# Three of sixteen activation sums of a block: from VectorE subtractions to in-place adding DMAs

## The chip, the cores and the metric

The kernel runs on one core of a Trainium2 chip. The metric is device time in microseconds (us) of one launch. Before the change three runs gave 2333.43, 2333.84 and 2334.41 us, median 2333.84.

## What is computed

A lightweight convolution (each of 8 heads has 7 softmax-normalised taps, causal in the sequence) runs over 8 x 4096 tokens of 192 channels, and its result goes through a two-layer block with a SiLU between, all in float32:

```python
w = np.exp(weight - weight.max(-1, keepdims=True)); w = w / (w.sum(-1, keepdims=True) + 1e-09)
x = einsum('hk,bskhg->bshg', w, windows_of_7(x_padded)).reshape(32768, 192)
h = x @ w_in            # 192 -> 2048
g = h * (1 / (1 + np.exp(-h)))
out = g @ w_out         # 2048 -> 192
```

## The kernel before

**Blocks.** The 32768 tokens are 32 blocks of 1024, each two token halves `n` of 512. The 2048 inner channels are four groups `j` of 512, and a group is two halves `a` of two chunks `e` of 128. Block 0 is multiplied plainly (`up_plain`, `down_plain`); blocks 1 to 31 use schemes with fewer multiplications.

**Up.** Per block and group, 20 products (`P0` to `P19`, `product`, L656) of 64 rows each go into PSUM banks named b0 to b6. Between them stand copies and additions in `micro`: copies `k`, `u`, `h` on ScalarE (L687, L689), or on VectorE (L678, L681) if their name is in `ON_DVE`; additions `i`, `j` on VectorE (L694); and the SiLU `S13` to `S20` on ScalarE (L691), which writes g. g lies in SBUF as eight tiles `gs[b, j, a]` of 128 partitions x (n, e, 512); a tile is written anew in each block. `of(a, n)` is one half of such a tile, 128 x 1024. `S14` and `S16` write `of(0, 1)`; `S18` and `S20` write `of(1, 1)`.

**Sums.** A 2x2 scheme for the second multiplication needs four sums of g per group, `t.j0` to `t.j3` (`sum_g`, L711), so 16 a block, each one VectorE subtraction of 128 x 1024. They go into two rotating tiles, `t0` (sums 0 and 1) and `t1` (sums 2 and 3). Sum 0 reads `of(0, 1)` and `of(0, 0)`; sum 1 reads `of(1, 1)` and sum 0; sum 2 reads `of(1, 1)` and `of(0, 1)`; sum 3 reads `of(1, 0)` and sum 1.

**Down.** `out_slot` (L746) issues slots `Di.je` (i from 0 to 5, group j, chunk e), each of four products side by side on 32 columns of the array. They accumulate in banks acc0 to acc5. Slot 3 alone reads sum 2 (beside sum 3). Slot 5 moves a quarter of the columns. A float32 matmul is two instructions in the profile, so a `P` is 2 of them and a `D` is 8.

**Merge and store.** `merge` (`M1` to `M7`, L823, VectorE) adds the accumulators, with ScalarE copies `x`, `y`, `z` (L803 to L811) beside it; `o` (`turn_out`, L835) transposes; `st` stores through SP's queue.

**The next block's input** is made meanwhile: `ld` loads through SP's queue, `i` transposes (L548, VectorE), `ha` takes over the last columns of the block before (a small copy on Pool, L569, and a DMA on SP's queue), `v` convolves (18 instructions on VectorE, L582; three on ScalarE, L579), `sp` spreads the result by DMAs (L599) and `w` adds windows (L607), which the products read.

**Order.** The order is written out by hand: `START` for the first blocks and `PLAN` for each later one are lists of tokens, and every engine executes its own in list order. `+` names the next block's token, `-` and `=` in START those of one and two blocks earlier. The lists fix the order within an engine only; between engines it is semaphores. `dp` are pieces of block 0's `down_plain` (L765), `cp` copies of its result, `go` half passes of `combine` (weight sums on VectorE), `co` calls of `combine_out` (sums of w_out). `D3` slots of the last block wait until the token `CLOSING` is done, and `finish` closes the last block. `TOUCHES` counts the uses after which a tile is free again.

Pool has little to do after the weights are made: the small `ha` copy once a block. DMAs issued by Pool exist only at the start (`w_other<-w_own`, L456).

Of the kernel before, what the change touches and what calls it, by code (L numbers as in the profile page):

```python
# [12 lines left out]
ALU = mybir.AluOpType  # L13
# [4 lines left out]
def kernel(  # L18
# [12 lines left out]
    nc = tc.nc  # L31
# [16 lines left out]
    NJ = NM // 2  # L48
# [41 lines left out]
    )  # L90
    START = (
# [1031 lines left out]
```

## Time and profile before

| what | us |
|---|---|
| profiled execution, whole | 2334.11 |
| its span, first to last instruction | 2332.4 |
| matmuls (PE) busy | 2324.2 (100%) |
| VectorE (DVE) busy | 2178.5 (93%) |
| ScalarE (ACT) busy | 1330.8 (57%) |
| Pool busy | 53.7 (2%) |
| the sums, VectorE L711, 496 instructions | 302.5 + 300.6 |
| granted TensorE clock | 0.999 |

A share near 100% for PE says that some matmul is nearly always in flight; it does not say that the matmuls follow each other as closely as they can, because the end of each is modelled and covers the start of the next. So time is read from the distances between starts. In groups of instructions, a row reads: line, engine, operation, output tile <- inputs, shape, count, then total busy time and mean ns of one, then the engine's idle time before these and what ended it. PEld is the weight load of a matmul, which runs ahead of it. POOLq and SPq are the issuing of DMAs.

### The profile page before, as it was taken

The page shows a single profiled execution, that of the slowest core. Times are in us where ns is not written, and L with a number is a line of the kernel's source. Part 1 is how long each engine was busy: PE and PEld are TensorE (multiplying, and loading weights), DVE is VectorE, ACT ScalarE, POOL GpSimd, SP SyncE. Part 2 cuts the span into 40 slices and gives each one's busy share as a digit, 9 for nine tenths or more (in the row PEclk, how much of TensorE's full clock was granted, in tenths as well). Part 3 has the DMA queues.
Part 4 walks back from the last instruction along what each step waited for, and adds up shares of the span by engine and source line. Part 5 has one row for each costly group of instructions (what it writes and reads, how often), then busy time and mean ns, then how long its engine had stood idle before and what let it go on. Part 6 is the DMA issues. An engine that isn't in the chain of part 4 may idle for free.

```text
span 2332.4 us, 43764 instructions
## 1 busy us (share of the span) xinstructions
PE 2324.2 (100%) x17382; PEld 921.5 (40%) x17382; DVE 2178.5 (93%) x3045; ACT 1330.8 (57%) x2523; POOL 53.7 (2%) x84
## 2 busy tenths in 40 slices
PE   9999999999999999999999999999999999999998
PEld 5344343334333344333344333443334433334433
DVE  8999999999999999999999999999999999999996
ACT  5356655566654576545666555665457654566654
POOL 4200000000000000000000000000000000000000
PEclk9999999999999999999999999999999999999999
DMA  7211221212212222212122122221221221212211
GB/s 159 57 37 26 53 53 30 50 32 49 53 37 43 44 37 53 45 37 50 28 53 53 30 49 35 46 53 39 40 51 30 53 49 34 50 28 53 53 33 22
DMA packets 451246, 106.55 MB, mean 46 GB/s; under 512 B 423585, under 2 KB 428705, under 8 KB 451041
## 3 DMA queue, kind: packets, MB, share of 16 engines
q1 hardware_dynamic: 447392, 101.78, 23.3%
q8 instruction: 136, 2.23, 0.4%
q0 software_dynamic: 448, 1.58, 0.3%
q10 hardware_dynamic: 3200, 0.39, 0.1%
q14 instruction: 70, 0.57, 0.1%
HBM read 31.46 MB, written 25.17 MB: 24 GB/s over the span
## 4 chain that ended last, share of the span: by engine, by line
PE 95%; DVE 1%; SPq 0%; DMA 0%; issue 0%; ACT 0%; ACTq 0%
PE ps L746 48%; PE ps L656 47%; SPq L599 0%; DVE t L711 0%; DMA nat<-in_x_dram 0%; DVE win L607 0%; DVE u L678 0%; DVE w_other L257 0%; SPq L289 0%; DVE w_own L257 0%; DVE cmb L257 0%; DVE ps L694 0%; ACT u L257 0%; DVE g L694 0%; DVE wx L257 0%
## 5 line engine op out<-in xcount | busy, mean ns | idle before, releaser
L656 PE MATMUL ps<-win,w_own 64*128 64x512 f32 x1488 | 661.4, 598 | 0.8 <-DVE win L607 0.5
L746 PE MATMUL ps<-g,wo 128*32 128x512 f32 x2976 | 661.5, 592 | 0.0
L746 PE MATMUL ps<-t,wo 128*32 128x512 f32 (+1 forms) x4528 | 511.3, 447 | 0.0
L656 PE MATMUL ps<-dup,w_own 64*128 64x512 f32 x1240 | 492.5, 594 | 0.2 <-ACT ps L689 0.2
L746 PE MATMUL ps<-t,wx 128*32 128x512 f32 x2976 | 484.7, 592 | 0.0
L691 ACT ACTIVATE g<-ps 128x512 f32<-128x512 f32 x620 | 367.1, 599 | 186.6 <-DVE g L694 113.9
L656 PE MATMUL ps<-dup,w_other 64*128 64x512 f32 x1240 | 460.0, 595 | 0.0
L656 PE MATMUL ps<-win,w_other 64*128 64x512 f32 x992 | 444.6, 595 | 0.0
L694 DVE TENSOR_TENSOR g<-g,ps 128x512 f32<-128x512 f32 x496 | 331.3, 683 | 54.4 <-PE ps L656 35.4
L582 DVE SCALAR_TENSOR_TENSOR nat<-xt,turned,nat 128x512 f32<-128x512 f32 x558 | 378.2, 746 | 3.9 <-ACT nat L579 1.6
L808 ACT COPY yx<-ps 32x512 f32<-32x512 f32 x150 | 84.3, 579 | 516.7 <-PE ps L746 514.9
L656 PEld LDWEIGHTS ps<-win,w_own 64*128 64x128 f32 x1488 | 246.6, 186 | 211.4 <-issue 120.3
L711 DVE TENSOR_TENSOR t<-g,t 128x1024 f32<-128x1024 f32 x248 | 302.5, 1220 | 16.9 <-PE ps L746 9.6
L711 DVE TENSOR_TENSOR t<-g 128x1024 f32<-128x1024 f32 x248 | 300.6, 1212 | 13.3 <-PE ps L746 13.1
L746 PEld LDWEIGHTS ps<-t,wo 128*32 128x32 f32 x4528 | 175.1, 110 | 248.4 <-issue 189.9
L694 DVE TENSOR_TENSOR ps<-u,ps 128x512 f32<-128x512 f32 x372 | 255.3, 687 | 11.8 <-ACT u L687 5.2
L656 PEld LDWEIGHTS ps<-dup,w_own 64*128 64x128 f32 x1240 | 195.5, 186 | 142.7 <-issue 77.2
L746 PE MATMUL ps<-g,wx 128*32 128x512 f32 x1488 | 245.7, 592 | 0.0
L691 ACT ACTIVATE g<-g 128x512 f32<-128x512 f32 x372 | 220.8, 625 | 27.1 <-DVE g L694 23.6
L689 ACT ACTIVATE ps<-ps 128x512 f32<-128x512 f32 x372 | 214.5, 584 | 36.0 <-DVE ps L694 19.0
L746 PEld LDWEIGHTS ps<-g,wo 128*32 128x32 f32 x2976 | 173.1, 110 | 148.0 <-issue 147.2
L656 PEld LDWEIGHTS ps<-dup,w_other 64*128 64x128 f32 x1240 | 167.8, 186 | 131.3 <-ACT ps L689 50.3
(102 smaller groups left out, 1826.3 us busy)
## 6 DMA issues: line engine op xcount, KB each, us to landing
dup<-nat SPq DMA_DIRECT2D x221, 128.0 KB, 2.3
nat<-in_x_dram SPq DMA_DIRECT2D x382, 64.0 KB, 2.4
out_dram<-t SPq DMA_DIRECT2D x372, 64.0 KB, 2.0
win<-nat SPq DMA_DIRECT2D x124, 128.0 KB, 2.4
raw<-in_moe_w_out_dram SPq DMA_DIRECT2D x8, 384.0 KB, 3.9
raw<-in_moe_w_in_dram SPq DMA_DIRECT2D x12, 192.0 KB, 5.0
w_other<-w_own POOLq DMA_DIRECT2D x8, 192.0 KB, 5.6
raw<-in_moe_w_in_dram SPq DMA_DIRECT2D x6, 128.0 KB, 3.4
```

What stands on the lines that cost most here:

```text
L582: nc.vector.scalar_tensor_tensor(out=dst, in0=src, scalar=tap, in1=dst, op0=ALU.mult, op1=ALU.add)
L656: nc.tensor.matmul(at(b, "bank", to, g), raw(g, w, e), rows(slot_of(b, x_), e), start=first, stop=True, skip_group_check=True,)
L689: pin(nc.scalar.activation(seen[to], seen[u], AF.Copy, scale=-1.0))
L691: pin(nc.scalar.activation(seen[to], seen[u], AF.Silu, scale=float(sign)))
L694: pin(nc.vector.tensor_tensor(seen[to], seen[u], seen[v], op=op))
L711: pin(nc.vector.tensor_tensor(t[i // 2][:, i % 2, :], u, v, op=ALU.subtract))
L746: nc.tensor.matmul(acc[SQ * q : SQ * q + SQ, to], lhs[:, e, SQ * k : SQ * k + SQ], rhs[:, e, ts(q, TB // 4) if i == 5 else to], start=firs ...
L808: pin(nc.scalar.copy(to, acc(3 * (name[0] == "x") + k)[n:P, :]))
```

## The change

Sum 2 of groups 0, 1 and 2 is no longer a VectorE instruction: Pool's queue issues a DMA that reads `of(1, 1)`, 128 x 1024 float32 (512 KB), and adds it into `of(0, 1)` where that lies. Group 3, and groups 2 and 3 of the last block, do the same addition on VectorE in place. `t1` thus holds sum 3 only, and slot 3 reads `of(0, 1)` of the g tile instead.

Such a DMA can add but not subtract, so signs move: all sums are now additions, `combine_out` swaps an addition and a subtraction in the weights, and `M2`, `M5` and three additions of `finish` become subtractions, with the same operands.

`PLAN` and `START` are replaced by other orders of (but for the five tokens that change the side of a block's border) the same tokens, `ON_DVE` grows from ten names to twelve, `TOUCHES` of `t1` goes from 8 to 7, and `CLOSING` becomes `S16.3`.

```diff
-    ON_DVE = ('h15.3', 'h18.0', 'k12.0', 'k12.1', 'k12.3', 'k8.0', 'u10.1', 'u10.2', 'u10.3', 'u6.2')
-    CLOSING = "S14.3"
+    ON_DVE = ('h15.3', 'h18.2', 'k12.0', 'k12.1', 'k5.3', 'k8.0', 'k8.1', 'k9.0', 'k9.3', 'u4.2', 'u4.3',
+              'u6.2')
+    BY_DMA = (0, 1, 2)
+    CLOSING = "S16.3"
...
-        t = {k: sums_of(b, j, k) for k in ((0,), (0,), (1,), (0, 1))[i]}
+        t = {k: sums_of(b, j, k) for k in ((0,), (0,), (), (0, 1))[i]}
+        if i == 2:
+            to, u = of(0, 1), of(1, 1)
+            if j in BY_DMA and not (b == NB - 1 and j >= NJ // 2):
+                pin(nc.gpsimd.dma_start(out=to, in_=u, accum_op=ALU.add))
+            else:
+                pin(nc.vector.tensor_tensor(to, u, to, op=ALU.add))
+            return
         u, v = (
             (lambda: (of(0, 1), of(0, 0))),
             (lambda: (of(1, 1), t[0][:, 0, :])),
-            (lambda: (of(1, 1), of(0, 1))),
+            None,
             (lambda: (of(1, 0), t[0][:, 1, :])),
         )[i]()
-        pin(nc.vector.tensor_tensor(t[i // 2][:, i % 2, :], u, v, op=ALU.subtract))
+        pin(nc.vector.tensor_tensor(t[i // 2][:, i % 2, :], u, v, op=ALU.add))
...
-            7: lambda: (a_[1][0], t(2)),
+            7: lambda: (a_[1][0], gs[b, j, 0][:, 1]),
...
-            "M2": lambda: (c[3], c[1], acc(1)[0:n, :]),
+            "M2": lambda: (c[3], acc(1)[0:n, :], c[1]),
...
-            "M5": lambda: (c[3], c[2], acc(4)[0:n, :]),
+            "M5": lambda: (c[3], acc(4)[0:n, :], c[2]),
...
-        pin(nc.vector.tensor_tensor(out_, u, v, op=ALU.add))
+        op = ALU.subtract if name in ("M2", "M5") else ALU.add
+        pin(nc.vector.tensor_tensor(out_, u, v, op=op))
```

The part of PLAN that the sums stand in, before and after (VectorE's and Pool's tokens of it alone; those in brackets are now Pool's):

```
before  +i15_11.1 +u10.2 +t.00 +u6.2 +j6.2 +i15_f.2 +t.02 +u10.3 +j6.3 +t.01 +t.03 +i15_f.3 +j10.2 +i18_10.2
        +j10.3 +i18_10.3 +ze.0 +t.10 +i15_11.2 +i17_f.2 +i17_f.3 +t.11 +t.13 +t.20 +t.21 +i15_11.3
        (next list) i.1 i.0 i.2 t.12 t.23 t.22 v.01 v.21 ...
after   +i15_11.1 +k5.3 +u6.2 +h18.2 +j6.2 +i15_f.2 +t.00 +j6.3 +k9.3 +t.01 +i15_f.3 +t.03 +j10.2 +i18_10.2
        [+t.02] +ze.0 +j10.3 +i18_10.3 +i17_f.2 +t.10 +i17_f.3 +i15_11.2 [+t.12] +t.11 +t.13 +i15_11.3
        +t.20 +t.21 [+t.22] (next list) i.1 i.0 i.2 t.23 v.21 v.22 ...
```

And TensorE's tokens of the same part:

```
before  ... +P13.3 +P10.3 +P4.3 +P15.2 +P9.3 +P15.3 +D3.01 +D2.01 +P12.2 +P14.2 +P12.3 +P14.3 +D3.00 +D4.00
        +D5.01 +D4.01 +D5.00 +D2.00 +D2.11 +D2.10 +D4.10 ... (next list) D3.11 D5.10 D3.10 D5.20 ... D3.20 D3.21
after   ... +P13.3 +P10.3 +P12.2 +P15.2 +P4.2 +P15.3 +D2.01 +D4.01 +D2.00 +P12.3 +P14.2 +P4.3 +P14.3 +D4.00
        +D5.01 +D3.00 +D5.00 +D0.30 +D3.01 +D4.10 +D1.31 +D4.11 +D2.11 +D2.10 +D0.00 +D0.21 +D3.10 ...
        (next list) D5.20 D4.21 D4.20 D3.21 ... D3.20
```

In START, the three tokens `go.0`, `go.2`, `go.1` stand on VectorE before the window `w.5` of block 1 and `go.3` some instructions behind it; before the change it was `go.2`, `go.3`, `co.0` before and `go.0` behind, `go.1` further on.

More of the change, by code (lines that the diff above doesn't have):

```diff
@@ L232 @@
                't0': 7,
-               't1': 8,
+               't1': 7,
                'acc0': 10,
@@ L494, in combine_out @@
         x_ = [wx[j][:, i, :, :] for i in range(3)]
-        vec.tensor_tensor(x_[0], a_(1, 0), a_(1, 1), op=ALU.add)
+        vec.tensor_tensor(x_[0], a_(1, 0), a_(1, 1), op=ALU.subtract)
         vec.tensor_tensor(x_[1], x_[0], a_(0, 0), op=ALU.subtract)
-        vec.tensor_tensor(x_[2], a_(0, 1), x_[1], op=ALU.subtract)
+        vec.tensor_tensor(x_[2], a_(0, 1), x_[1], op=ALU.add)
         vec.tensor_tensor(a_(1, 0), a_(0, 0), a_(1, 0), op=ALU.subtract)
@@ L934, in part, with add @@
             return t[SQ * k : SQ * k + SQ, :]
-        def add(out_, u, v):
-            vec.tensor_tensor(out_, u, v, op=ALU.add)
+        def add(out_, u, v, op=ALU.add):
+            vec.tensor_tensor(out_, u, v, op=op)
         def store(i, cols):
@@ L976, in finish @@
         act.copy(part(y, 2), acc(2)[n:P, :])
-        add(c[1], c[2], acc(1)[0:n, :])
+        add(c[1], acc(1)[0:n, :], c[2], ALU.subtract)
         add(c[0], c[0], y[0:n, :])
@@ L981, in finish @@
         add(c[1], c[1], acc(4)[0:n, :])
-        add(c[3], c[2], acc(4)[0:n, :])
+        add(c[3], acc(4)[0:n, :], c[2], ALU.subtract)
         act.copy(part(x_, 1), acc(4)[n:P, :])
@@ L994, in finish @@
                     )
-            add(c[3][:, cols], c[3][:, cols], p7[0:n, cols])
+            add(c[3][:, cols], c[3][:, cols], p7[0:n, cols], ALU.subtract)
             add(c[2][:, cols], c[2][:, cols], p7[0:n, cols])
```

190 rows, old and new, of tables (PLAN, START) are left out of this document.

## The prediction

> **What bounds the kernel now.** I read the page's first part, then the chain that ended last in order of time, to see at what pace the blocks follow each other; then the timeline of TensorE, VectorE and ScalarE over one block, to see where that pace is not the matmuls' own. The page, and four pieces of the chain:
>
> ```profile
> PE 2324.2 (100%) x17382; PEld 921.5 (40%) x17382; DVE 2178.5 (93%) x3045; ACT 1330.8 (57%) x2523; POOL 53.7 (2%) x84
> PE 95%; DVE 1%; SPq 0%; DMA 0%; issue 0%; ACT 0%; ACTq 0%
> ...
> 858.21 34.50 PE ps L746 x368
> 892.72 33.29 PE ps L656 x151
> 926.00 1.85 PE ps L746 x16
> 927.86 1.92 PE ps L656 x8
> 929.77 34.50 PE ps L746 x368
> ```
>
> Columns of the pieces: start, length, what. Block follows block at 71.56 us (929.77 - 858.21), all of it TensorE. In the timeline a product starts 0.429 us after the one before and a full slot takes twice that, 0.858. A block has 80 products (34.3 us), 40 full slots (34.3) and 8 quarter slots (1.7): 70.4 us. What is left, 1.17 us a block, is all that any edit off TensorE can win there: 36 us in 31 blocks, 1.5%. Most of it is the four changes a block between products and slots; the new list has four as well (its products stand in two runs of 76 and 4). What remains is waits. One is seen in TensorE's rows, its weight loads and the two engines behind it (products `P13.3`, `P10.3`, and the end of the first run at `P15.3`):
>
> ```profile
> 1565.29 1.22 DVE L711 TENSOR_TENSOR t<-g 128x1024 f32<-128x1024 f32 x1
> 1566.42 0.68 DVE L678 COPY u<-ps 128x512 f32<-128x512 f32 x1
> 1567.07 0.70 DVE L694 TENSOR_TENSOR ps<-u,ps 128x512 f32<-128x512 f32 x1
> 1567.86 1.07 ACT L689 ACTIVATE ps<-ps 128x512 f32<-128x512 f32 x2 [0.22 <-DVE ps L694]
> 1568.49 0.18 PEld L656 LDWEIGHTS ps<-dup,w_own 64*128 64x128 f32 x1 [0.64 <-ACT ps L689]
> 1568.51 0.68 PE L656 MATMUL ps<-win,w_own 64*128 64x512 f32 x1
> 1569.03 0.59 PE L656 MATMUL ps<-win,w_own 64*128 64x512 f32 x1
> 1570.74 0.59 PE L656 MATMUL ps<-dup,w_other 64*128 64x512 f32 x1
> 1570.88 0.59 PE L656 MATMUL ps<-dup,w_own 64*128 64x512 f32 x1
> 1571.40 1.07 PE L746 MATMUL ps<-t,wo 128*32 128x512 f32 x8
> 1574.64 0.59 PE L656 MATMUL ps<-win,w_own 64*128 64x512 f32 x1
> 1575.17 1.07 PE L746 MATMUL ps<-t,wo 128*32 128x512 f32 x8
> ```
>
> The first three rows are `t.02`, `u10.3` and `j6.3` without a gap; ScalarE's `k9.3` waits for `j6.3`, `P13.3`'s weights wait for `k9.3`, and 1568.51 to 1569.03 is 0.52 instead of 0.43. So a sum that this change takes off VectorE stands in a chain that holds TensorE, for 0.09 us. At the end of the first run the second half of `P15.3` starts 0.14 late, and the way to the slots is 0.66 (1570.74 to 1571.40), against 0.53 at the end of the second (1574.64 to 1575.17): 0.13 more. VectorE's own share over a whole block, 1503.68 to 1575.24, is 67.41 us of 71.56 in the stretches view: 4.1 us free.
>
> For the adding DMA the nearest rows are Pool's eight early transfers, and plain ones of SP:
>
> ```profile
> w_other<-w_own POOLq DMA_DIRECT2D x8, 192.0 KB, 5.6
> raw<-in_moe_w_out_dram SPq DMA_DIRECT2D x8, 384.0 KB, 3.9
> nat<-in_x_dram SPq DMA_DIRECT2D x382, 64.0 KB, 2.4
> ...
> L456 POOL DMA_DIRECT2D w_other<-w_own x8: 518/639/876, 22.6 to 42.3; - x8
> DMA to landing us min/median/max: 3.2/5.6/6.7
> ```
>
> **The change part by part.**
>
> *VectorE loses 92 sums* (31 blocks x 3, less one), of 1.22 us by the row of L711: 112 us. `ON_DVE` gives it two copies more a block, 62 x 0.68 = 42 us, and takes 62 x 0.59 = 37 us from ScalarE. VectorE ends 70 us lighter, some 90% busy. None of that is on TensorE's path by itself; it counts only where a wait on VectorE holds a matmul.
>
> *The wait at P13.3.* In the new order `t.02` and `u10.3` are gone ahead of `j6.3`, `k9.3` follows it on VectorE, and `P13.3` stands eight products behind `P6.3`, whose result `j6.3` adds, instead of six. From `i15_11.1` to `j6.3` VectorE has six instructions instead of seven, with one sum of 1.2 us less. I take the wait as gone: 30 x 0.09 = -2.7 us (bounds 0 and -2.7).
>
> *The late second half of P15.3.* It shows 0.13 x 30 = 3.9 us. ScalarE's `k17.3` is next to it, in a queue that loses two copies a block; what holds it I can't tell for sure. Bounds 0 and -3.9, I take half: -2.0.
>
> *Late blocks.* In the chain the distance from one L746 x368 piece to the next is 71.56 in most blocks and more in a few (1073.67 - 1001.34 = 72.33; 1503.68 - 1431.75 = 71.93); the excess over 71.56 adds up to 2.0 us. The one at 1489 to 1497 runs through VectorE, with both `t.00` and `t.02` in it. Bounds 0 and -2.0, I take -1.5.
>
> *The DMAs: 92 issues on Pool's queue.* Nothing is queued behind them there but `ha`'s small copy, 0.51 us, which has to be done when `i.2` and its DMA are; `t.22` is issued when `t.20` is done, at about 1580.9, and `ha` is needed after 1583.5, so it passes. The issuing itself takes Pool 0.65 us and nobody waits for Pool. Landing: from 192 KB at 5.6; from 64 to 384 KB SP's rows grow by 1.5 us, 4.7 ns a KB, so 512 KB adds 320 x 4.7 = 1.5, and reading the destination too adds 512 x 4.7 = 2.4: 9.5 us. Bounds: 5.6 (if the bytes cost nothing), and 5.6 x 512/192 = 14.9 (if all of it goes by bytes); I take 9.5, since the rows of SP say that most of a transfer is fixed. When is it needed? `t.10` ended at 1574.78; the new order puts `i17_f.2` ahead of it, so 1575.3. The second run of products ends where it did plus one slot (three slots stand in the gap instead of two), less the waits: `D4.00` at 1576.0. Before `D3.10` come eleven full slots and two quarters, 9.9 us: 1585.9. That leaves 10.6 us, so 9.5 is hidden, with 1.1 to spare. For `t.02` it is about the same: `t.00`, which ended at 1563.45, has four more instructions of 0.65 ahead of it and ends near 1566.1, `D3.00` starts at 1577.1, 11.0. For `t.22` it is some 19 (`D3.21` stands 17 full slots behind `D3.10`). The DMA engines are 23% busy; loads, spreads and stores each wait in SP's queue for their own inputs long before they are needed, except the spreads just ahead of the windows, and those run 10 us after `t.22` has landed. Price: 0, by this cover.
>
> That this cover is thin, one sentence of the Trainium skill says too: "SBUF — State Buffer", "Summary: rules for kernel authors", holds that making the descriptors of a Pool-issued DMA is starved while VectorE runs in its faster two-port modes. The rows show eight issues of 518 to 876 ns beside a VectorE that was 53.31 of the first 60 us busy, so such a delay is at most 0.36 us each here, and by the rule the landing would be 9.9, still inside 10.6.
>
> *A tile that is free later.* `of(0, 1)` is now read by `D3` until TensorE is through; the next block's `S14`, `S16` write it more than 30 us on. Price 0.
>
> *Signs.* An addition for a subtraction is the same VectorE instruction with the same operands: 0.
>
> *START.* `w.5`, which `P1.0` needs, now stands behind 21 half-pass instructions of the weight sums instead of 15 and `co.0` (four of 0.35): 21 x 0.44 - (15 x 0.44 + 1.4) = +1.2 us; against that 7 of them (3 us) leave the place between `w.5` and the first copies, and two transposes (1.4) come in. `go.3` (3 us) comes behind `j4.0`, earlier than `go.1` did. Bounds -1.5 and +3.2; VectorE is 39.42 of 40 us busy from 60 to 100, so this shows. I take +1.0.
>
> *Sum.* The profiled execution took 2334.11 us, 0.27 over the median: 2334.11 - 2.7 - 2.0 - 1.5 + 1.0 = 2328.9, and against the median 2328.6.
>
> **The rivals.**
>
> *No change that counts* (within 0.2%, 4.7 us, about what a measurement of this kernel can tell from none). VectorE was not the bound, 4.1 us a block were free, and its relief becomes idle time: P13.3 is held by the next thing (`k9.3` itself), the half of P15.3 stays, and START costs 1 to 3 us. For it: only 0.22 us a block is named above. Then 2334 - 2.7 + 2 = 2333.
>
> *The adding DMA lands after TensorE asks for it* (slower). Place: `D3.10`, and `D3.00` with it. It decides at 10.6 us from the end of `t.10` to the landing: each us beyond costs 31 us in all, since TensorE has nothing else in its order. For it: an addition in flight is in no row of this trace, and the bound of 14.9 lies beyond. Against it: the median of 5.6 and the 6.7 at most, in a stage where the DMA engines were 72% busy. At 12 us: +1.4 x 31 - 5 = +38, 2372.
>
> *The new order makes a wait of its own* (slower). `t.13` ends at 1575.3 + 1.3 + 2.4 = 1579.0 and `D4.10` starts at 1579.9, which leaves 0.9 (1579.7 and 1580.8 before, 1.1); and `D0.30`, at 1578.1, waits for `S17.3`, whose input now comes behind `t.10` on VectorE. If either slips past that by 0.4 us in each block: 31 x 0.4 = +12, less 5: 2341.
>
> *More than named.* All waits but the four changes go, 0.5 us a block: 2334 - 15 - 2 = 2317.
>
> **How the numbers follow.** Forecast, with the last rival at its far end: 0.42, own range 2321 to 2329. No change: 0.25, 2329 to 2338. Late DMA: 0.20. A wait of the new order: 0.13, 2339 to 2350. The range 2321 to 2350 holds all but the far end of the first (0.03) and the late DMA beyond 11.3 us (0.15). Faster 0.42, same 0.25, slower 0.33.
>
> **What would show it.** Right: pieces of the chain at 71.3 to 71.5 us a block; the L711 row of `t<-g` down by 92; no wait of PEld or PE by a DMA at L746; 1568.51 to 1569.03 again 0.43. Wrong: idle time of PEld at L746 ended by a DMA whose issue is at the new Pool line, with landings over 10.6 us; or the block's pace unchanged and VectorE's idle time 2 us larger; or, for START, less matmul work started between 100 and 110 us than the 7.1 us of now (by the slots above).

## The result and the profile after

The changed kernel takes 2339.69 us (median of 10 runs, 2338.83 to 2340.97); the kernel before, run beside it, 2334.14 us (2333.13 to 2335.45). The ratio is 1.0024, with a 95% interval of 1.0014 to 1.0034: slower by 5.5 us, where 2328.6 was forecast. The profiled execution took 2339.14 us, its span 2337.4 us, against 2332.4 us before. Lines of the page after, parts 1, 4 and 5:

```profile
PE 2328.0 (100%) x17382; PEld 954.1 (41%) x17382; DVE 2122.7 (91%) x3015; ACT 1292.0 (55%) x2461; POOL 136.1 (6%) x176
PE 95%; DVE 4%; issue 0%; DMA 0%; SPq 0%; ACT 0%; DVEq 0%; ACTq 0%
L584 DVE SCALAR_TENSOR_TENSOR nat<-xt,turned,nat 128x512 f32<-128x512 f32 x558 | 391.2, 747 | 68.0 <-ACT nat L581 62.5
```

VectorE is lighter, as meant, and yet its share of the chain that ended last rose from 1% to 4%. The row to see first is L584, the convolution `v`: VectorE now idles 68.0 us in front of it. (What this idle time is worth, the experiments have to say.) The adding DMAs themselves land in 4.6 us (median); the new DMA line, by its own view:

```profile
L710 POOL DMA_DIRECT2D g<-g x92: 853/862/972, 134.4 to 2295.8; - x92
DMA to landing us min/median/max: 4.5/4.6/6.3
```

**Where the 5.0 us of the span went.** I took the start of `P7.0` in each block as its border. From the span's start to the block that begins at 320 us the changed kernel is 0.4 us quicker; the 27 blocks after that take 1937.8 us against 1934.2 (+3.6); from the last block's `P7.0` to the end it is 80.0 against 78.2 (+1.8).

In the middle two things oppose each other. The shortest block, which is also the commonest, fell from 71.56 to 71.49 us, since the forecast wait at `P13.3` is gone: 27 x 0.07 = -2.0. But the excess of the longer blocks over that rose from 2.1 to 7.6 us in all, +5.5. Before, 4 of the 27 are over 0.2 us longer than the shortest; after, 13 are. The stretches view of one undisturbed block of after (columns: length, then busy time and instructions of PE, PEld, DVE, ACT and POOL, clock, DMA share, GB/s):

```profile
1514.26:1585.75 71.49, 71.49 (x547) 28.94 (x543) 65.23 (x92) 40.53 (x77) 3.21 (x4) 1.00 0.35 64
```

VectorE is busy for 65.23 us of a block (67.41 before), the DMA engines for 35% of it.

**The late blocks, read in the trace.** The next block's input ends with the transpose `i.2`; then `ha.0`'s DMA on SP's queue brings 4.5 KB (the halo), and only then can ScalarE start the first convolutions `v.20`, `v.00`, whose results VectorE's `v.21` and `v.01` add to. The timeline of before, at a typical block whose `i.2` ended at 939.09:

```profile
939.01 1.18 DVE L711 TENSOR_TENSOR t<-g 128x1024 f32<-128x1024 f32 x1
940.12 1.21 DVE L711 TENSOR_TENSOR t<-g,t 128x1024 f32<-128x1024 f32 x1
941.25 1.22 DVE L711 TENSOR_TENSOR t<-g 128x1024 f32<-128x1024 f32 x1
942.38 2.19 DVE L582 SCALAR_TENSOR_TENSOR nat<-xt,turned,nat 128x512 f32<-128x512 f32 x3
...
941.20 1.95 ACT L579 ACTIVATE nat<-xt,turned 128x512 f32<-128x512 f32 x3 [2.28 <-DVE t L711]
```

VectorE fills the time of the halo's flight with `t.12`, `t.23` and `t.22`, and goes on at 942.38 without a gap. After, `t.12` and `t.22` are DMAs, and `t.23` stands there alone. A late block and the one behind it (their `i.2` ended at 867.61 and 940.33):

```profile
867.54 1.22 DVE L720 TENSOR_TENSOR t<-g,t 128x1024 f32<-128x1024 f32 x1
872.61 1.54 DVE L584 SCALAR_TENSOR_TENSOR nat<-xt,turned,nat 128x512 f32<-128x512 f32 x2 [3.85 <-ACT nat L581]
871.86 1.95 ACT L581 ACTIVATE nat<-xt,turned 128x512 f32<-128x512 f32 x3 [7.40 <-DMA xt<-xt]
...
940.25 1.23 DVE L720 TENSOR_TENSOR t<-g,t 128x1024 f32<-128x1024 f32 x1
943.48 2.87 DVE L584 SCALAR_TENSOR_TENSOR nat<-xt,turned,nat 128x512 f32<-128x512 f32 x4 [2.00 <-ACT nat L581]
942.72 1.95 ACT L581 ACTIVATE nat<-xt,turned 128x512 f32<-128x512 f32 x3 [5.55 <-DMA xt<-xt]
```

In the second VectorE idles 2.0 us; in the first the halo is late, ScalarE starts 4.25 us after `i.2` instead of 2.4, and VectorE idles 3.85. I call a halo late when ScalarE's first `v` starts over 2.9 us after the end of `i.2`: 2 of 27 blocks before, 5 of 28 after. The waits view gives the sums over the run, first of before, then of after (us in total, times, longest):

```profile
ACT nat L579 <- DMA xt<-xt: 30.8, 11, 7.1
DVE nat L582 <- ACT nat L579: 2.5, 3, 0.9
```

```profile
ACT nat L581 <- DMA xt<-xt: 124.2, 22, 7.5
DVE nat L584 <- ACT nat L581: 63.3, 30, 4.0
```

What follows behind the convolution has little room. In the new order `t.30` and `t.31` stand among the `v`, so `v.16` ends 17.9 us after `i.2` (15.6 before); its spread `sp.4` lands at 20.1, just when the window sum `w.0`, which reads it, is due at 20.13. Any delay then runs through `w`, `M`, `k12`, `j4.0` and `k5.0` to TensorE, which waits 0.34 us behind `P5.1` in 11 blocks of 28, and at `D5.31` and `D3.20` for up to 0.6 us in the blocks with a late halo.

**The last block.** There the slots `D3.x` are put off behind CLOSING, `D0.30` and `D1.31` are not done, and so `D4.10` comes early and finds `t.13` not made. The chain of after:

```profile
2296.45 1.15 DVE t L720
...
2297.62 1.24 DVE t L720
2298.90 10.52 PE ps L755 x104
```

TensorE starts `D4.10` 2.1 us late: that is the +1.8 at the end.

### The profile page after: what moved, and what is told of

Same layout as the page of the kernel before. It is cut to its first block, busy times and chain, and to the rows that moved or that the text cites. A ratio compares the mean times of both kernels' runs of the same rounds, so it can differ in the third digit from the quotient of the medians.

```text
span 2337.4 us, 43887 instructions
## 1 busy us (share of the span) xinstructions
PE 2328.0 (100%) x17382; PEld 954.1 (41%) x17382; DVE 2122.7 (91%) x3015; ACT 1292.0 (55%) x2461; POOL 136.1 (6%) x176
## 4 chain that ended last, share of the span: by engine, by line
PE 95%; DVE 4%; issue 0%; DMA 0%; SPq 0%; ACT 0%; DVEq 0%; ACTq 0%
PE ps L755 48%; PE ps L658 47%; DVE two L259 2%; DVE nat L584 1%; DVE mh L259 1%; DVE w_own L259 0%; DVE t L720 0%; SPq L291 0%; DMA dup<-nat 0%; DVE w_other L259 0%; DVE g L696 0%; DVE xt L550 0%; DVE wo L259 0%; DMA nat<-in_x_dram 0%; DVE win L609 0%
## 5 line engine op out<-in xcount | busy, mean ns | idle before, releaser
L755 PE MATMUL ps<-g,wo 128*32 128x512 f32 (+1 forms) x4512 | 913.1, 588 | 0.0
L755 PE MATMUL ps<-t,wo 128*32 128x128 f32 (+1 forms) x2992 | 528.3, 378 | 1.3 <-DVE t L720 1.3
L658 PE MATMUL ps<-dup,w_other 64*128 64x512 f32 x1240 | 505.0, 595 | 0.0
L755 PE MATMUL ps<-t,wx 128*32 128x512 f32 x2976 | 476.2, 594 | 0.0
L584 DVE SCALAR_TENSOR_TENSOR nat<-xt,turned,nat 128x512 f32<-128x512 f32 x558 | 391.2, 747 | 68.0 <-ACT nat L581 62.5
L755 PEld LDWEIGHTS ps<-g,wo 128*32 128x32 f32 x4512 | 232.3, 110 | 223.7 <-issue 213.2
L755 PE MATMUL ps<-g,wx 128*32 128x512 f32 x1488 | 250.4, 592 | 0.0
L658 PEld LDWEIGHTS ps<-dup,w_other 64*128 64x128 f32 x1240 | 194.0, 186 | 101.1 <-issue 56.8
L755 PEld LDWEIGHTS ps<-t,wo 128*32 128x32 f32 x2992 | 172.2, 110 | 136.6 <-issue 123.3
L755 PEld LDWEIGHTS ps<-t,wx 128*32 128x32 f32 x2976 | 115.6, 110 | 258.6 <-issue 211.6
L658 PEld LDWEIGHTS ps<-win,w_other 64*128 64x128 f32 x992 | 171.3, 186 | 115.4 <-issue 60.1
```

Source lines behind the costliest of these rows:

```text
L584: nc.vector.scalar_tensor_tensor(out=dst, in0=src, scalar=tap, in1=dst, op0=ALU.mult, op1=ALU.add)
L658: nc.tensor.matmul(at(b, "bank", to, g), raw(g, w, e), rows(slot_of(b, x_), e), start=first, stop=True, skip_group_check=True,)
L755: nc.tensor.matmul(acc[SQ * q : SQ * q + SQ, to], lhs[:, e, SQ * k : SQ * k + SQ], rhs[:, e, ts(q, TB // 4) if i == 5 else to], start=firs ...
```

## The experiments

Three theories. **Halo:** the adding DMA of `t.22`, which is in flight around the end of `i.2`, makes the halo late. **Order:** `t.30` and `t.31` ahead of `v.16` let `w.0` and `P5.1` wait. **Tail:** the last block. Against the first stands a rival: the DMA disturbs nothing, and what is missing is only the cover by VectorE's sums. Lengths of "27 blocks" below are measured as above; 27 of the shortest would be 1930.2 us.

**Old order, three DMAs.** The changed kernel with the lists of before. In the first multiplied block, the old START lets `t.02` be added in place before `t.00` reads that half, so this one sum is of other numbers; the instructions are the same.

```diff
-        "ld.2 ld.1 ld.0 i.1 i.0 i.2 ha.0 v.20 v.00 t.23 D5.20 D4.21 v.10 D4.20 v.21 v.22 v.01 "
+        "ld.1 i.1 ld.0 i.0 ld.2 i.2 t.12 D3.11 D5.10 t.23 D3.10 t.22 D5.20 D5.21 D4.21 ha.0 D4.20 "
...
-    CLOSING = "S16.3"
+    CLOSING = "S14.3"
```

> The changed kernel with the lists of before (PLAN, START, ON_DVE, CLOSING), so the three DMAs and the signs alone. Theory O (the new order costs the time, the DMAs are hidden): the block's shortest period falls under 71.56 us, because a sum leaves the chain ahead of P13.3, and no block waits at D5.31, D3.20 or P5.1 more often than before; 2329 to 2332 us. Theory D (the adding DMAs disturb the small halo DMA and the spreads on the shared DMA engines): blocks that are late by 0.3 us or more in 10 of 28 as in the changed kernel, 2336 to 2340.

Measured: 2333.74 us, ratio 0.9997 (0.9989 to 1.0006). So 112 us of sums less on VectorE are worth nothing by themselves: the shortest block is 71.56 again and the 0.085 us at `P13.3` are still there, though `t.02` is gone from VectorE. Over the whole run the DMAs cost nothing in this order either; but the halo is late in 8 blocks of 27 instead of 2, and in the trace these 27 take 1935.8 us against 1934.2 (the stretch ahead of them is 1.4 us shorter). The old order bears most of a late halo, I think because `t.30` to `t.33` stand between `v.16` and `w.0`.

**The two sums moved, three times.** First `t.30` and `t.31` behind `v.16`, alone:

```diff
-        ... v.04 t.30 v.26 y1.0 v.05 v.06 sp.7 t.31 sp.8 v.14 sp.0 sp.10 v.15 D2.31 D2.30 v.16 y2.0 t.33
+        ... v.04 v.26 y1.0 v.05 v.06 sp.7 sp.8 v.14 sp.0 sp.10 v.15 D2.31 D2.30 v.16 t.30 t.31 y2.0 t.33
```

> The changed kernel with t.30 and t.31 moved in PLAN behind v.16, so that the convolution ends as early as before; one sum alone still covers the halo DMA. Theory O: v.16 ends about 15.6 us behind the end of i.2 (17.9 in the changed kernel), the window w.0 no longer waits for its spread, the 0.34 us waits at P5.1 go from 13 blocks to 5 or fewer (those with a late halo stay late): 2335.5 to 2337. Theory D: the spreads themselves land late, the waits stay: 2339 to 2340.

Measured: 2415.92 us, ratio 1.0349 (1.0334 to 1.0363), which says nothing on the theory: `D2.31` and `D2.30` read `t.31`, and my edit put the sum behind them. They read what the tile held before, and `t.31` has to wait until TensorE has done so, each block. Then both ahead of the convolution, where VectorE idles:

```diff
-        ... t.23 D5.20 D4.21 v.10 D4.20 v.21 ... v.04 t.30 v.26 y1.0 v.05 v.06 sp.7 t.31 sp.8
+        ... t.23 t.30 t.31 D5.20 D4.21 v.10 D4.20 v.21 ... v.04 v.26 y1.0 v.05 v.06 sp.7 sp.8
```

> The changed kernel with t.30 and t.31 moved in PLAN ahead of v.21, behind t.23, so that three sums cover the halo DMA as before, and the convolution ends as early as before. Theory O: both kinds of late block go, all but a few periods are 71.49; 3.4 us less than with the sums behind the convolution, 2332 to 2334 (the wait for t.13 in the last block, 2 us, stays). Theory D: no better than with the sums behind the convolution.

Measured: 2535.37 us, ratio 1.0863 (1.0848 to 1.0878). Its waits view tells why:

```profile
DVE t L720 <- PE ps L755: 244.8, 32, 9.3
```

`t.31` waits until 10.7 us after `i.2` for a tile that slots of the groups before still read, the whole convolution waits behind it, and TensorE then waits 4.5 us at `D4.30`. The gap can't be filled with these sums. Last, behind `v.16` with their two readers moved along:

```diff
-        ... sp.7 t.31 sp.8 v.14 sp.0 sp.10 v.15 D2.31 D2.30 v.16 y2.0 t.33
+        ... sp.7 sp.8 v.14 sp.0 sp.10 v.15 v.16 t.30 t.31 D2.31 D2.30 y2.0 t.33
```

> The changed kernel with t.30 and t.31, and the slots D2.31 and D2.30 that read them, moved in PLAN behind v.16; TensorE's own order and everything else stay. Theory of the order (the two sums among the convolutions let v.16 end 17.9 us after the last input transpose instead of 15.6, so the spread that w.0 waits for lands when w.0 is due and every hiccup of SP's queue delays w.0, M, k12, j4.0 and P5.1): v.16 ends at about 15.7 us, w.0 begins at 20.1 to 20.4 us in all but a few blocks (median 20.9 now), the 0.34 us waits at P5.1 fall from 11 blocks of 28 to 4 or fewer, the mean block from 71.78 to about 71.6 us, and the time by 3 to 5 us, to 2335 to 2337. Theory of the late halo transfer (the adding DMA beside it alone makes blocks late): the halo comes as late as before, D5.31 and D3.20 wait as often, and the time stays within 1 us of 2339.7. Theory that only the last block's wait counts: no change.

Measured: 2340.78 us, ratio 1.0025 (1.0015 to 1.0034); no gain. `v.16` does end at 15.6, and the 0.34 us behind `P5.1` are gone from every block. But the 27 blocks take 1941.0 us, because TensorE now waits at `D2.31`, for `t.31`, which has only 0.2 to 0.4 us to spare there (the same row has 13.6 us in the changed kernel, 2.2 of them in the last block):

```profile
PEld ps L755 <- DVE t L720: 22.6, 39, 2.2
```

It waits 0.5 to 1.9 us in exactly nine blocks, and those are the nine in which the halo is late (9 of 9); the others take 71.49. So the order theory is right about `P5.1` and wrong about the price: moving the sums only moves the place at which a late halo is paid.

**The last block.** Three more kinds of slot put off to CLOSING:

```diff
-        if b == NB - 1 and token[:3] == "D3." and (b, CLOSING) not in did:
+        late = ("D3.", "D2.1", "D4.1", "D5.1")
+        if b == NB - 1 and token.startswith(late) and (b, CLOSING) not in did:
```

> The changed kernel, and in the last block D4.1x, D2.1x and D5.1x wait for the closing token as the D3 do, so that TensorE does not meet t.13 early. Theory: the 2.1 us wait for t.13 in the last block goes: 2337.5 to 2338.2. Rival: the wait passes to what comes next in the list (t.11 or the last chunks of g): 2339 to 2340.

Measured: 2338.54 us, ratio 1.0018 (1.0009 to 1.0027), 1.2 us below the changed kernel. From the last `P7.0` to the end it is 77.7 us instead of 80.0, and in the chain no VectorE stands between the pieces of TensorE any more; the slots are one piece:

```profile
2297.42 32.00 PE ps L755 x392
```

The tail theory holds, with 2.3 us in the trace; the halo was late in 7 blocks of that execution, and its 27 blocks are 1.9 us longer. Together with the move above:

```diff
+        "... v.15 v.16 t.30 t.31 D2.31 D2.30 y2.0 ..."
...
+        late = ("D3.", "D2.1", "D4.1", "D5.1")
```

> The same move, and in the last block D4.1x, D2.1x and D5.1x put off behind CLOSING as D3 is. If the middle's loss (3.6 us) is the order of the sums and the end's (1.9 us) is TensorE's wait for t.13 at D4.10, both go: 2333.5 to 2336. If only one of the two is right: about 2336 to 2338.5.

Measured: 2338.38 us, ratio 1.0016 (1.0007 to 1.0025), 2.4 us below the move alone; the halo is late in 7 blocks of 28. Only one of the two cures works, as long as the halo is late.

**The third sum back on VectorE.**

```diff
-    BY_DMA = (0, 1, 2)
+    BY_DMA = (0, 1)
...
-        "ld.2 ld.1 ld.0 i.1 i.0 i.2 ha.0 v.20 v.00 t.23 D5.20 ... +D2.21 +t.22 +D1.20 +S16.3"
+        "ld.2 ld.1 ld.0 i.1 i.0 i.2 ha.0 v.20 v.00 t.23 t.22 D5.20 ... +D2.21 +D1.20 +S16.3"
```

> The changed kernel with t.22 on VectorE again, right behind t.23, where VectorE waits for the halo now; t.02 and t.12 stay DMAs. VectorE has 1.9 us of idle time there, so v.21 begins at 3.0 us after the last input transpose as before. Theory of the late halo transfer: v.00 late (over 2.9 us) in 2 or 3 blocks of 28 instead of 5 to 7, since no adding DMA runs beside the halo, the waits at D5.31 and D3.20 go, and the time falls by 2 to 3.5 us, to about 2336.5. Theory of the order of t.30 and t.31: w.0 late and P5.1 waiting as often as now, the time within 1 us of 2339.7. If the halo is late as often without the DMA, what delays it is something else (the loads of the next input, whose place the order also changed).

Measured: 2335.56 us, ratio 1.0003 (0.9994 to 1.0012), 4.1 us below the changed kernel and no longer different from before. The halo is late in 1 block of 27, and ScalarE's first `v` starts at 2.08 us (median) as before the change, not at 2.31; the 27 blocks take 1933.1 us instead of 1937.8. The 0.34 us behind `P5.1` are still there in 6 blocks. With the last block's slots put off too, without and with the move of the two sums:

```diff
-    BY_DMA = (0, 1, 2)
+    BY_DMA = (0, 1)
...
+        late = ("D3.", "D2.1", "D4.1", "D5.1")
```

> The version with all three edits, with t.30, t.31, D2.31 and D2.30 back in the changed kernel's places: only t.22 on VectorE behind t.23, and the last block's slots put off. Theory that the order of t.30 and t.31 is a loss of its own: the 0.34 us waits at P5.1 are there in 5 to 10 blocks and the time is 2 to 3 us above 2331.1. Theory that it costs nothing once the halo comes on time: within 1 us of 2331.1.

Measured: 2333.02 us, ratio 0.9992 (0.9983 to 1.0000); the 0.34 us behind `P5.1` are there in 4 blocks.

```diff
-    BY_DMA = (0, 1, 2)
+    BY_DMA = (0, 1)
...
+        "... v.15 v.16 t.30 t.31 D2.31 D2.30 y2.0 ..."
...
+        late = ("D3.", "D2.1", "D4.1", "D5.1")
```

> All three edits together. If the three losses are the order of t.30 and t.31, the late halo and the last block's wait, the shortest block of 71.49 us holds nearly everywhere: about 2330 to 2333, below both kernels. If one of the three is not a cause, 2333 to 2337.

Measured: 2331.10 us, ratio 0.9985 (0.9976 to 0.9993): quicker than before. Its 27 blocks take 1930.9 us against 1932.0 without the move, so the order of the two sums is worth about 1 us in the trace and 2 us between the medians once the halo comes on time, less than the 2 to 3 that I expected; the two intervals overlap.

**DMA or cover?** The third sum on VectorE both takes a DMA away from the halo and fills VectorE's gap. First I meant to put a DMA of the same size back into the quickest version, at its old moment:

```diff
         pin(nc.vector.tensor_tensor(t[i // 2][:, i % 2, :], u, v, op=ALU.add))
+        if (j, i) == (2, 0) and b < NB - 1:
+            pin(nc.gpsimd.dma_start(out=of(0, 0), in_=of(1, 1), accum_op=ALU.add))
```

> The version with all three edits (2331.1 us), with an adding DMA of 512 KB put back at the moment at which t.22's ran (behind t.20, on Pool's queue, same source), into the half that t.20 has just read instead of t.22's; VectorE still makes t.22 behind t.23. The half then holds a number that is not the reference's, and no instruction waits for the DMA that didn't have eight microseconds to spare. Theory that the adding DMA beside the halo makes the halo late: v.00 over 2.9 us after the last input transpose in 5 to 9 blocks of 27 again (1 without the DMA), and with TensorE waiting 0.5 to 1.5 us in each, 2333 to 2338. Theory that only the missing cover on VectorE mattered: the halo on time as in the version without, and the time within 1 us of 2331.1.

Measured: 2343.23 us, ratio 1.0036 (1.0024 to 1.0049), but not for either reason. The 27 blocks behind the first run at the pace of the version without the DMA (mean of all blocks 71.53 us for both), and the halo is late in 1 of 27; the loss, some 12 us, lies in START, between the first product of block 1 (101.3 us) and that of block 2 (188.9, against 176.7 without the DMA). There the DMA is issued at 158.14, and a SiLU waits for it on ScalarE:

```profile
162.64 0.63 ACT L693 ACTIVATE g<-g 128x512 f32<-128x512 f32 x1 [12.18 <-DMA g<-g]
```

In the later blocks the waits view shows that the DMA missed its moment:

```profile
POOL g L722 <- PE ps L757: 260.1, 28, 11.1
```

Slots that still read the half held it back, 9.3 us a block on Pool's queue, until 2.1 us after `i.2`; its packets start 3.6 us after `i.2`, those of `t.22` in the changed kernel 1.2 us before it. It ran behind the halo, so it doesn't test the theory as meant; it shows that a DMA of this size 4.8 us later does no harm to the halo. That suggested the cleaner test: all three sums by DMA, the move and the last block's slots as above, and `t.22`'s DMA held on Pool's queue until `t.23` has ended. VectorE gets nothing to fill the gap.

```diff
+                if j == 2 and (b, "t.23") in did:
+                    pin(nc.gpsimd.tensor_copy(spare, held_at[b, "t1", j][:, 1, 0:1]))
                 pin(nc.gpsimd.dma_start(out=to, in_=u, accum_op=ALU.add))
...
-        "ld.2 ld.1 ld.0 i.1 i.0 i.2 ha.0 v.20 v.00 t.23 D5.20 ... +D2.21 +t.22 +D1.20 +S16.3"
+        "ld.2 ld.1 ld.0 i.1 i.0 i.2 t.23 t.22 ha.0 v.20 v.00 D5.20 ... +D2.21 +D1.20 +S16.3"
```

> The version with the two sums and their slots behind the convolutions and the last block's slots put off (2338.4 us; halo over 2.9 us in 7 blocks), all three sums by DMA, with one edit: t.22's DMA is held on Pool's queue, by a copy of one column of t.23's result, until t.23 has ended, 1.1 us after the last input transpose, so that its packets run behind the halo's and not beside them. VectorE gets no work in the gap. Theory that the adding DMA beside the halo makes the halo late: v.00 late in 1 to 3 blocks, no wait at D2.31, and 2331 to 2333. Theory that what helped was only that VectorE's sum covered the wait: the halo late in 7 blocks and 2337.5 to 2339.5. If the DMA, landing some 7 us after the transpose, is too late for D3.21 at 17.5 us: slower than 2339.5.

Measured: 2330.74 us, ratio 0.9987 (0.9978 to 0.9996), against 1.0016 for the same kernel with the DMA at its old moment. The timeline of a block whose `i.2` ended at 866.6 (Pool, ScalarE, VectorE):

```profile
867.89 0.18 POOL L712 COPY spare<-t 128x1 f32<-128x1 f32 x1 [8.38 <-DVE t L723]
868.83 1.95 ACT L582 ACTIVATE nat<-xt,turned 128x512 f32<-128x512 f32 x3 [5.37 <-DMA xt<-xt]
869.59 3.65 DVE L585 SCALAR_TENSOR_TENSOR nat<-xt,turned,nat 128x512 f32<-128x512 f32 x5 [1.83 <-ACT nat L582]
```

The DMA's packets now start 3.2 us after `i.2`, 4.4 later than before. ScalarE starts at 2.1 to 2.2, the halo is late in 1 block of 28, and 24 of the 27 blocks take the shortest time, 71.49 us. VectorE still idles here, 1.83 us in the block shown: the cover was not what mattered, the DMA at the wrong moment was. So the idle time in front of the convolution, the row that stood out in the page after, was in itself no loss; this version still has 55.5 us of the 68.0, and none of the others is quicker.

Over all versions: where `t.22`'s DMA runs shortly before or beside the halo (the changed kernel and six experiments), the halo is late in 48 blocks of 195; where it doesn't (before and six experiments), in 10 of 190.

**No DMA at all.** The version with all three edits (2331.10 us), with `t.02` and `t.12` on VectorE too:

```diff
-    BY_DMA = (0, 1)
+    BY_DMA = ()
```

> The version with all three edits, with t.02 and t.12 on VectorE too, in their places in PLAN: no adding DMA is left. VectorE has 2.3 us more a block, 69 of 71.5 us. If the two DMAs that are left are worth their place, the sums stand in VectorE's way behind the products of a block and TensorE waits: some tenths to 2 us in each block, 2335 to 2380. If the order alone is what made this version quick, 2329 to 2333.

Measured: 2393.47 us, ratio 1.0250 (1.0236 to 1.0264), above both of my ranges. The commonest block is 73.52 us, with TensorE waiting for sums behind `P14.3` (0.61) and `D4.10` (0.67), and for the convolution's followers further on:

```profile
PEld ps L755 <- DVE t L720: 55.8, 72, 1.6
```

So the DMAs are a condition of the new order as it is written, not a gain of their own: without them it is 62 us slower, and with them the old order is as quick as before. Other places for the sums in the new order were not tried.

## Why the prediction was wrong, point by point

The forecast was 2328.6 us in a range of 2321 to 2350, with 0.33 on slower. The time lies in the range, on the side that I held less likely.

- **VectorE's relief**: right in kind, 91% busy against "some 90%", 65.23 us a block. In size it is 55.8 us in the page (2178.5 to 2122.7), not 70: busy time of the convolution's row grew by 13.0 (378.2 to 391.2). That the relief counts for nothing by itself was right too; the old order with the DMAs shows it.
- **The wait at `P13.3`, -2.7**: right in size, -2.0 over the 27 blocks that were compared. Of the reasons I gave, sums that leave VectorE are not enough: the old order without them keeps the wait. What removes it is the new list (`u10.3` off VectorE, `k9.3` on it, or the places of `P13.3` and `t.02`); these were not told apart.
- **The late half of `P15.3`, -2.0**: wrong. The way from `P15.3` to the slots is 0.656 us in every block after, as it was before (but for one block). I had put half of a wait whose holder I couldn't name into the sum.
- **The DMAs, "Price: 0, by this cover"**: this is the step that failed. I asked when each DMA must have landed, and what waits behind it on Pool's queue ("nothing is queued behind them there but `ha`'s small copy", "it passes"). Of SP's queue I took loads, spreads and stores, and left out the halo: a DMA on SP's queue, in flight just after `i.2`, when `t.22`'s DMA runs. So I put at nothing what the DMA does to another transfer. The runs show a price: with `t.22` off the DMA the 27 blocks take 4.7 us less, and with the DMA held until the halo is through, the same kernel takes 2330.74 us instead of 2338.38.
- **Late blocks, -1.5**: wrong in sign, +5.5. I looked for what the removed sums had held up, not for what the change would hold up itself: the late halo above, and with it the order of `t.30` and `t.31` (0.34 us behind `P5.1` in 11 blocks), which is worth some 1 us once the halo comes on time.
- **Spreads, "10 us after `t.22` has landed"**: true of the DMA, but no cover against the order: `sp.4` moved from a place with 5 us of sums behind it to one where it lands when `w.0` is due.
- **The landing of 9.5 us, bounds 5.6 and 14.9**: wrong; 4.6 at the median, below the lower bound, and 6.3 at most. So the cover of 10.6 us was thick, not thin, and the rival of the late DMA, with 0.20, did not come: no row of the waits view after has TensorE wait for a DMA at the slots (L755). I had added the destination's bytes in full and a slope of SP's rows on top of the median of Pool's row. The sentence on the Trainium skill's "SBUF — State Buffer" hung on the same term: by the rule of its "Summary: rules for kernel authors" Pool's descriptors would be held up while VectorE runs in its faster two-port modes. Here 92 issues took 853 to 972 ns beside a VectorE that was 91% busy, no more than 0.12 us apart, so this run shows no delay that comes and goes with what VectorE does; one that is the same each time it can't show.
- **START, +1.0**: measured -0.4 up to 320 us, inside its bounds.
- **The end**: not in the sum, +1.8. The list was read for the blocks in a row; what it does where tokens are left out, in the last block, was not.
- **The rival "a wait of the new order's own", 2341, 0.13**: its time is near the measured 2339.7, but that is luck. The wait that it names, `D4.10` for `t.13` in each block, comes in the last block alone; the +5.5 comes mostly from the late halo, which it doesn't name.
- **The signs**: those that I had named for being right came (71.49 us a block, 0.43 behind `P13.3`, 92 sums less, no wait for the adding DMA), and the time went the other way. All of them look at the commonest block or at the DMA's own landing, and none at the blocks that are longer.

The measured terms add up: -0.4 - 2.0 + 5.5 + 1.8 = +4.9, against +5.0 in the spans.

## What to carry to other kernels

A large transfer can cost something though it lands in time: look at what small transfers are in flight when it is started, and start it a few microseconds later if nothing needs it yet. Here, with the sums and the last block in order, 0.18 us on Pool turned 0.16% slower than before into 0.13% quicker. An engine that loses work begins to idle at waits that the work had hidden; that names the wait, but is not yet a loss, as the quickest version shows. And read a hand-written order once more for its first and last round.

## What the runs showed of the hardware

An adding DMA of 512 KB within the on-chip memory, issued by Pool, lands in 4.6 us (4.5 to 6.3), less than the 192 KB copies by the same queue at the kernel's start (median 5.5 in the same run; there the DMA engines were 72% busy, by the trace of before). The Trainium skill's fit for a Pool-issued DMA ("DMA: Bandwidth & Descriptors", "Anatomy of one DMA — SWDGE (gpsimd) path": 2.0 us and the bytes at 436 GB/s) gives an estimate of 3.2 us for it; the trace has 4.6. What the other 1.4 us are, no run here shows.

A transfer of 4.5 KB on SP's queue comes some 0.2 us later at the median, and up to 2 us later in one block of four, when such a DMA runs just before or beside it (2.31 against 2.08 us to ScalarE's start in the changed kernel; 48 of 195 blocks late against 10 of 190). That fits the same page of the Trainium skill, "Issuing engines are not separate DMA queues", which says that DMAs of all engines run on the same 16 DMA engines and interleave.

Which blocks are hit can be read from the DMA packets of the traces. Beside the kernel's own transfers there are packets that the profile calls `instruction` (in the changed kernel 136 on q8 and 70 on q14, mostly of 16 and 8 KB); by their name they load the program. The DMA view of 3.7 us around `i.2`, first of the late block shown above, then of the one behind it, which has no such row:

```profile
q8 instruction: 1, 0.02, 1.6%
xt<-xt SPq DMA_DIRECT2D x1, 4.5 KB, 4.1
...
xt<-xt SPq DMA_DIRECT2D x1, 4.5 KB, 2.1
```

Taken over 28 blocks of each of the 14 traces (one more in some than was counted above), 59 halos are late, and in each of these blocks a packet of this kind is in flight at some time between 1.5 us before and 2.2 us after the end of `i.2`. Of the 230 blocks without one, none is late. With one, 49 of 79 are late where `t.22`'s DMA runs just before or beside the halo, and 10 of 83 where it doesn't. In the late block above that packet runs from 2.10 to 3.04 us after `i.2`, and of the 384 packets of 24 bytes that the halo and its neighbour `tail` consist of, 24, a sixteenth, start from 3.03 us on, the others by 2.3; in the block behind all start by 2.3. That looks like one of the 16 DMA engines being held. It is read from the traces alone: no run here moves the loading of the program.
